# Attention and MLP in one kernel: the high half-precision parts of q, k and v made on DVE instead of POOL, with eleven scheduling constants replaced

## The chip, the core and the metric

The kernel runs on one core of one Trainium2 chip. A core has a matrix engine (PE), a vector engine (DVE), a scalar engine (ACT), a further vector processor (POOL) and an engine that here does nothing but issue DMAs (SP). Each engine runs its own list of instructions strictly in order and waits on semaphores for the others. The metric is device time in microseconds (us) of one execution.

## The reference

Batch 8, 12 heads, 448 positions, head size 64, so a model width of 768; hidden width 3072; float32 in and out.

```
scores = q @ k^T / sqrt(64) - log(448)          # per batch and head
x      = sigmoid(scores) @ v                     # heads laid side by side: 448 x 768
u      = x + (x^T @ U @ V)^T                     # rank 32, mixes the 448 positions
out    = u + relu(u @ w_ch1) @ w_ch2             # 768 -> 3072 -> 768
```

There is no softmax: the sigmoid needs no sum over a row.

## The kernel before, in words

**Numbers.** PE multiplies float16. To keep near-float32 precision, a float32 matrix x is scaled by a power of two s and split into a high part hi = float16(s*x) and a low part lo = float16(s*x - hi). A product then takes three matmuls: hi*hi, hi*lo and lo*hi. Making hi takes one input tensor (a multiplication by s); making lo takes two (x and hi). Batches 0 and 1 do their attention in plain float32, which is slower on PE but needs no split; batches 2 to 7 use the three-matmul form.

**Work and stages.** A "pair" is two heads of one batch, 448 positions: it loads q, k and v, computes scores (line 503), a sigmoid on ACT (line 590), a split of the sigmoid (lines 611 and 363) and the product with v (lines 514 and 518). Six pairs make a batch, after which the low-rank mixing follows (`mix` and `mix_half`). In stretches:

- about 0 to 300 us: attention of batches 0 and 1, and `decode`: the weights come as 64-bit words, are turned to float32, split, and stored to DRAM (`scratch`).
- about 300 to 950 us: the MLP of batches 0 to 3 (`ffn_in` line 838, `ffn_out` line 858), while the attention of batches 2 to 7 runs in between.
- about 950 us to the end: the MLP of batches 4 to 7, two batches at a time, by a scheme that multiplies quarters of the matrices with seven products in place of eight (`in_quad`, `out_quad`, product at line 1031). It needs sums of weight quarters, which `quarter_sums` makes: four additions and four more on POOL (lines 917 and 921), a cast on ACT (line 924), a subtraction on DVE (line 925) and a store. One buffer holds the sums, so a group on POOL starts only when the subtraction of the group before it is done. Eight groups run before 950 us, sixteen after.
- `far_forms` makes the sums of u for the first two of those batches ahead of time and stores them to DRAM (`ufar`, line 974); `near_forms` loads them back (line 998).

In `in_quad`, each product's results are combined and split again on DVE for the next stage. Near its end stands a row of seven DVE instructions that mostly read two tensors from SBUF (lines 1060, 363, 363, 1069, 1069, 1069, 363). The text calls this row a **burst**.

**What sets the order.** Nothing is emitted where it is written. Each step is registered with `op(engine, cost, function, reads, writes, position)`. `Plan.order` then walks a nominal clock: it always takes the operation that could start earliest by the nominal costs, and among those ready on one engine the one with the smallest position. That list, fixed at build time, is the order of each engine. Two more rules matter. An operation with `port=True` may not overlap another such one in the nominal clock: POOL operations with inputs have it, and so do the DVE operations registered through `dve2`; those of `in_quad` and `out_quad` are registered through `dve`, without it. And tiles come from rings of buffers, granted in that nominal time: `stg`, which holds the six parts of q, k and v of a pair, has two buffers.

**The preparation of a pair** (batches 2 to 7, function `pair`): ACT bounds q, k and v (line 420); the three bounds go by DMA through DRAM to every partition (`far`, `row`); DVE takes the largest (line 399), POOL computes inverse scales (`inv`, and the small factors `c` and `cv`), DVE the scales (line 403). Then, on POOL, the high parts of k, q and v are made by `scaled` (line 360 of the helper `ts`), and on DVE the low parts by `rest` (line 363).

The table of constants at lines 59 to 67 sets positions: `BEFORE`, `PREP`, `MIX_2`, `A_OFF` and so on shift the positions of attention, preparation, mixing and the split of the sigmoid; `ROOM0` and `ROOM` the nominal room left between batches; `U_STEP` and `STEP_K` the spacing of `far_forms` and of `quarter_sums`.

Of the kernel before, what the change touches and what calls it, by code (L numbers as in the profile page):

```python
# [32 lines left out]
ALU = mybir.AluOpType  # L33
# [22 lines left out]
FORMS = {1: (0,), 2: (1,)}  # L56
MM = 0.190

ROOM0, ROOM, AHEAD, BEFORE, PACE = 42.52, 45.6, 46.05, 25.79, 0.95
PREP, BOUNDS, VALUES, SECOND, MIXED = 14.886, 8, 1.353, 2.168, 6.146  # L60
LOW_POOL = ()
MIXED1, MIX_1 = 6.47, 3.6
MIX_2, EV_IN, EV_OUT, A_OFF = 1.824, 21.322, 5.63, 0.0
START, DECODE = 59.033, 39.61
U_AT, U_STEP = 4.779, 5
LEAD, SUMS, STEP_K, STEP_I, FFN_LEAD = 35.115, 18.57, 22.57, 8.637, 4.0
ORDER = "iiiioiooiioiooiioiooiooo"


# [19 lines left out]
class Plan:  # L89
# [13 lines left out]
    def op(self, eng, cost, fn, reads=(), writes=(), pos=0.0, slack=0.0, land=0.12, after=(), port=False):  # L103
        deps = set(after)
        for k in reads:
            deps.update(self.wrote.get(k, ()))
        for k in writes:
            deps.update(self.wrote.get(k, ()))
            deps.update(self.read.get(k, ()))
        i = len(self.ops)  # L110
        for k in reads:
            self.read.setdefault(k, []).append(i)
        for k in writes:
            self.wrote[k], self.read[k] = [i], []
        tiles = []
        for k in (*reads, *writes):
            t = k[0] if isinstance(k, tuple) else k
            if isinstance(t, Tile) and t not in tiles:
                tiles.append(t)
                t.users.append(i)  # L120
                if t.at is None:
                    t.at = (pos, i)
        self.ops.append((eng, cost, fn, sorted(deps), pos, slack, land, tiles, port))
        return i
# [96 lines left out]
def fused_kernel(ctx: ExitStack, tc: tile.TileContext, q, k, v, wu, wv, w1, w2, out):  # L221
    nc = tc.nc
    B = q.shape[0]
    plan = Plan()
# [109 lines left out]
    def sm(name, n, ring_=3):  # L334
        if name not in small:
            small[name] = ring(name, ring_, [n], F32)
        return plan.tile(name, small[name])
# [7 lines left out]
    def dve2(cost, fn, reads, writes, pos):  # L345

        op("DVE", cost, fn, reads, writes, pos, port=True)
# [4 lines left out]
    def pool(cost, fn, reads, writes, pos, after=()):  # L352
        op("POOL", cost, fn, reads, writes, pos, after=after, port=bool(reads))
# [4 lines left out]
    def ts(eng, out, in_, s1, op0, s2=None, op1=None):  # L358
        kw = {} if op1 is None else {"op1": op1}
        eng.tensor_scalar(out=out, in0=in_, scalar1=s1, scalar2=s2, op0=op0, **kw)  # L360
# [4 lines left out]
    def scaled(out, in_, s):  # L365
        ts(nc.gpsimd, out, in_, s, ALU.mult, 1.0, ALU.mult)
# [159 lines left out]
    def pair(b, p, at, d):  # L526
        whole = b < WHOLE
        u32, mx = u32s[b], mxs[b]
        if b == 0:
            qk, v32, kqk = loads(b, p, at - 60.0)  # L530
        else:
            qk, v32, kqk = loads(b, p, at - d - (30.0 if whole else 32.0))
        tiles, keys = {}, []
        if whole:
            c, kc = 1.0 / math.sqrt(D), []

            def score_products():
                return [(qk.x[:, 1, :], qk.x[:, 0, :])]

            def value_products():  # L540
                return [(v32.x, lambda t, h: t.x[:, h * S : (h + 1) * S])]

            kscore, kvalue = kqk, [v32]
        else:
            prep = at - PREP
            st, ss = plan.tile("stg", STG), sm("ss", 3)
            for i in range(2):
                bound(lambda i=i: qk.x[:, i, :], S, lambda i=i: ss.x[:, i : i + 1], kqk[2 * i : 2 * i + 2], (ss, i), prep - BOUNDS, 0.73)
            bound(lambda: v32.x.rearrange("p a b -> p (a b)"), 512, lambda: ss.x[:, 2:3], [v32], (ss, 2), prep - BOUNDS, 0.82)
            s, inv = scale_by_dma(ss, [(ss, i) for i in range(3)], 3, "qkv", prep - BOUNDS + 1)  # L550
            cc, cv = sm("c", 1), sm("cv", 1)
            pool(0.5, lambda: ts(nc.gpsimd, cc.x, inv.x[:, 0:1], inv.x[:, 1:2], ALU.mult, 1.0 / math.sqrt(D), ALU.mult), [inv], [cc], prep + 1)
            pool(0.45, lambda: ts(nc.gpsimd, cv.x, inv.x[:, 2:3], 1.0 / A_UP, ALU.mult, 1.0, ALU.mult), [inv], [cv], prep + 1)

            def part(n):

                if n < 4:
                    n = (2, 3, 1, 0)[n]
                    return st.x[:, n * S : (n + 1) * S]
                return st.x[:, 4 * S + (n - 4) * 4 * P : 4 * S + (n - 3) * 4 * P].rearrange("p (a b) -> p a b", a=4)  # L560

            for i in (1, 0):
                ki = kqk[2 * i : 2 * i + 2]
                pool(0.7, lambda i=i: scaled(part(2 * i), qk.x[:, i, :], s.x[:, i : i + 1]), ki + [s], [(st, 2 * i)], prep + 2,
                     plan.wrote["decoded"])
                dve2(0.63, lambda i=i: rest(part(2 * i + 1), qk.x[:, i, :], s.x[:, i : i + 1], part(2 * i)),
                    ki + [s, (st, 2 * i)], [(st, 2 * i + 1)], prep + 3)
            pool(0.8, lambda: scaled(part(4), v32.x, s.x[:, 2:3]), [v32, s], [(st, 4)], prep + 6, plan.wrote["decoded"])
            dve2(0.75, lambda: rest(part(5), v32.x, s.x[:, 2:3], part(4)), [v32, s, (st, 4)], [(st, 5)], prep + 7)

            def score_products():
                kh, kl = st.x[:, S:], st.x
                return [(kh, part(0)), (kh, part(1)), (kl, part(0))]

            def half(t, x):

                n = t.x.shape[1]
                return t.x.bitcast(F16)[:, x * n : (x + 1) * n]

            def value_products():  # L580
                def side(x):
                    return lambda t, h: half(t, x)[:, h * S : (h + 1) * S]

                return [(part(4), side(0)), (part(5), side(0)), (part(4), side(1))]

            kscore, kvalue = [(st, i) for i in range(4)], [(st, 4), (st, 5)]
            c, kc = cc, [cc]

        def sigmoid(cost, out_, in_, rows, pos, kin, kout):
            act(cost, lambda: nc.scalar.activation(  # L590
                out_(), in_(), AF.Sigmoid, bias=bias_s[rows], scale=c if whole else c.x[rows]), kin + ["bias"] + kc, kout, pos)

        sc = {}
        for n, j in enumerate((3, 0, 1, 2)):
            here = at + (d * (n // 2) / SECOND if b else 0.0)
            if b == 0:
                sc = scores_of(b, (j,), score_products, kscore, here, b == 0 or b == 1 and p < 2)
            elif n % 2 == 0:
                sc = scores_of(b, ((3, 0), (1, 2))[n // 2], score_products, kscore, here, b == 0 or b == 1 and p < 2)
            a = tiles[j] = plan.tile(*(("a1", A1) if j == 3 else ("a2", A2)))  # L600
            to = a if whole else plan.tile(*(("t1", AT1) if j == 3 else ("t2", AT2)))
            for h in range(2):
                rows = rows_of(h) if j == 3 else slice(0, P)
                cols = slice(0, S) if j == 3 else slice(h * S, h * S + S)
                sigmoid(0.66 if whole else 0.72, lambda to=to, rows=rows, cols=cols: to.x[rows, cols],
                        lambda h=h, sc=sc, j=j, rows=rows: sc[j, h].x[rows, :S], rows, here, [sc[j, h]], [(to, h)])
            kto = [(to, h) for h in range(2)]
            if whole:
                keys += kto
                continue  # L610
            act(0.57 if j == 3 else 0.95, lambda a=a, to=to: nc.scalar.activation(half(a, 0), to.x, AF.Copy, scale=A_UP), kto, [(a, 0)], here + A_OFF)  # L611
            dve2(0.63 if j == 3 else 1.16, lambda a=a, to=to: rest(half(a, 1), to.x, A_UP, half(a, 0)), kto + [(a, 0)], [(a, 1)], here + A_OFF)
            keys += [(a, 0), (a, 1)]
        late = at + d * (VALUES if b else 1.0)
        av = values_of(b, value_products, tiles, keys + kvalue, late)
        ku = u32[p]
        act(0.63, lambda: nc.scalar.activation(u32[p].x, av.x[:, :S], AF.Copy, scale=1.0 if whole else cv.x),
            [av] + ([] if whole else [cv]), [ku], late)
        if b > 0:
            largest(lambda: u32[p].x, lambda: mx.x[:, p : p + 1], [ku], (mx, p), late)  # L620
# [671 lines left out]
```

## Time and profile before

| quantity | value |
|---|---|
| median of 3 runs | 1598.71 us (1597.11 to 1600.68) |
| profiled execution, its own time | 1600.42 us |
| profiled execution, span of the instructions | 1598.6 us |
| PE busy | 1563.9 us, 98% |
| DVE busy | 1163.3 us, 73% |
| ACT busy | 855.8 us, 54% |
| POOL busy | 385.4 us, 24% |
| chain of work that ended last | PE 82%, DVE 9%, DMA 4%, the rest below 3% each |

A row of a group reads: line, engine, operation, output<-inputs, shapes, count, then busy us, mean ns of one, idle time of the engine before them and what ended it. Matmul ends are modelled and overlap their successors, so "PE busy" says that work was in flight, not that each slot was used; what PE waited for stands in the view of waits.

### The profile page before, as it was taken

The numbers are of one execution on the slowest core, as the hardware profiler recorded it, in microseconds if no ns is written. First come the engines' busy times: TensorE is split into PE (matmuls) and PEld (weight loads), VectorE is DVE, ScalarE is ACT, GpSimd is POOL, SyncE is SP. The second block draws the span as 40 slices with busy tenths as digits, with TensorE's granted clock in tenths as the row PEclk, the third lists the DMA queues.
The fourth block names the chain that finished last, engine by engine and source line by source line (L and its number), as shares of the span: only waits on it lengthen the run. The fifth ranks groups of instructions, "written<-read, shape, count | busy, mean of one in ns | idle before, by whom it ended". The sixth has DMA issues, their size and how long they took to land.

```text
span 1598.6 us, 23902 instructions
## 1 busy us (share of the span) xinstructions
PE 1563.9 (98%) x8774; PEld 769.3 (48%) x8774; DVE 1163.3 (73%) x1887; ACT 855.8 (54%) x1553; POOL 385.4 (24%) x468
## 2 busy tenths in 40 slices
PE   8999999999999999999999999999998999999999
PEld 3344444444454444454444444544444545555554
DVE  3899898666766568767677776797888777565656
ACT  6667754567846679757877872332333514121210
POOL 0100002642213442211211210466665320000000
PEclk9999999999999999999999999999999999999999
DMA  8798896765665797866766648877676663333321
GB/s 246 246 319 280 293 310 209 277 209 144 166 191 147 241 220 215 206 189 181 218 178 200 175 146 255 261 246 221 206 230 219 219 223 130 131 105 119 124 104 70
DMA packets 217430, 322.53 MB, mean 202 GB/s; under 512 B 132832, under 2 KB 183392, under 8 KB 205024
## 3 DMA queue, kind: packets, MB, share of 16 engines
q1 hardware_dynamic: 217312, 321.01, 65.1%
q8 instruction: 68, 1.11, 0.3%
q14 instruction: 50, 0.41, 0.1%
HBM read 249.40 MB, written 77.42 MB: 204 GB/s over the span
## 4 chain that ended last, share of the span: by engine, by line
PE 82%; DVE 9%; DMA 4%; ACT 2%; SPq 1%; issue 1%; POOL 1%; ACTq 0%; DVEq 0%; POOLq 0%
PE bank L1031 28%; PE bank L838 18%; PE bank L858 18%; PE bank L503 8%; PE bank L518 5%; PE bank L514 2%; DVE us__88 L363 1%; DMA qk__99<-q_in 1%; DVE xnt L925 1%; DVE us__87 L1069 1%; PE bank L755 1%; SPq L747 1%; DMA forms<-xnt 1%; DMA far<-ss__213 1%; DVE h__94 L363 1%
## 5 line engine op out<-in xcount | busy, mean ns | idle before, releaser
L363 DVE SCALAR_TENSOR_TENSOR a<-at,a 128x896 f16<-128x896 f32 (+1 forms) x144 | 143.1, 1000 | 44.5 <-ACT a L611 44.3
L858 PE MATMUL bank<-h__94,w__92 128*128 128x448 f16 x864 | 173.1, 353 | 1.4 <-DVE a L363 0.9
L858 PE MATMUL bank<-h__93,w__91 128*128 128x448 f16 x864 | 173.1, 353 | 0.0
L611 ACT ACTIVATE a<-at 128x896 f16<-128x896 f32 (+1 forms) x144 | 123.1, 855 | 0.5
L838 PEld LDWEIGHTS <-w__89 128*128 128x128 f16 x864 | 82.8, 98 | 84.0 <-issue 9.3
L838 PEld LDWEIGHTS <-w__90 128*128 128x128 f16 x864 | 83.5, 98 | 82.5 <-issue 8.3
L858 PEld LDWEIGHTS <-w__92 128*128 128x128 f16 x864 | 82.4, 98 | 83.9 <-issue 10.6
L858 PEld LDWEIGHTS <-w__91 128*128 128x128 f16 x864 | 81.4, 98 | 82.3 <-issue 9.8
L1031 PEld LDWEIGHTS <-w__89 128*128 128x128 f16 x819 | 80.1, 98 | 80.0 <-issue 5.4
L921 POOL TENSOR_TENSOR w<-w 128x384 f32<-128x384 f32 x96 | 110.4, 1150 | 5.2
L1031 PEld LDWEIGHTS <-w__91 128*128 128x128 f16 x756 | 74.4, 98 | 74.5 <-issue 6.4
L1031 PEld LDWEIGHTS <-w__90 128*128 128x128 f16 x756 | 73.9, 98 | 73.7 <-issue 5.0
L1031 PEld LDWEIGHTS <-w__92 128*128 128x128 f16 x693 | 68.3, 99 | 69.5 <-issue 7.3
L917 POOL TENSOR_TENSOR w<-w 128x384 f32<-128x384 f16 x64 | 66.1, 1060 | 116.0 <-DVE xnt L925 62.1
L838 PE MATMUL bank<-us__87,w__90 128*128 128x448 f16 x432 | 86.5, 357 | 0.9 <-DVE ua__78 L363 0.9
L838 PE MATMUL bank<-us__87,w__89 128*128 128x448 f16 x432 | 85.0, 353 | 1.2 <-ACT h__93 L846 1.2
L838 PE MATMUL bank<-us__88,w__90 128*128 128x448 f16 x432 | 85.8, 353 | 0.0
L838 PE MATMUL bank<-us__88,w__89 128*128 128x448 f16 x432 | 85.6, 353 | 0.0
L590 ACT ACTIVATE at<-bank,bias_s,c__226 128x448 f32<-128x448 f32 (+1 forms) x96 | 67.0, 725 | 14.9 <-PE bank L503 11.2
L590 ACT ACTIVATE at<-bank,bias_s,c__224 128x448 f32<-128x448 f32 (+1 forms) x96 | 66.8, 724 | 8.0 <-PE bank L503 5.2
L590 ACT ACTIVATE at<-bank,bias_s,c__225 128x448 f32<-128x448 f32 (+1 forms) x96 | 66.3, 721 | 4.6 <-PE bank L503 2.5
L590 ACT ACTIVATE a<-bank,bias_s 128x448 f32<-128x448 f32 (+1 forms) x96 | 55.9, 630 | 10.7 <-PE bank L503 10.1
(1190 smaller groups left out, 3122.0 us busy)
## 6 DMA issues: line engine op xcount, KB each, us to landing
w<-w_in SPq DMA_DIRECT2D x48, 768.0 KB, 5.8
forms<-xnt SPq DMA_DIRECT2D x24, 768.0 KB, 4.2
w__89<-forms SPq DMA_DIRECT2D x13, 1344.0 KB, 6.0
w__90<-forms SPq DMA_DIRECT2D x12, 1344.0 KB, 6.2
w__91<-forms SPq DMA_DIRECT2D x12, 1344.0 KB, 5.9
w__92<-forms SPq DMA_DIRECT2D x11, 1344.0 KB, 6.0
forms<-scratch SPq DMA_DIRECT2D x144, 96.0 KB, 4.8
w__89<-scratch SPq DMA_DIRECT2D x9, 1536.0 KB, 7.7
```

The costliest lines, as they stand in the source:

```text
L363: nc.vector.scalar_tensor_tensor(out=out, in0=in0, scalar=s, in1=in1, op0=op0, op1=op1)
L503: nc.tensor.matmul(o, keys, y[rows_of(h)], start=i == 0, stop=i == n - 1)
L514: nc.tensor.matmul(av.x[:, :S], x[:, 3, :], y(tiles[3], 0), start=i == 0, stop=False, skip_group_check=True)
L518: nc.tensor.matmul(av.x[rows_of(h), :S], x[:, j, rows_of(h)], y(tiles[j], h), start=False, stop=j == 2 and i == n - 1, skip_group_check=True,)
L590: act(cost, lambda: nc.scalar.activation(out_(), in_(), AF.Sigmoid, bias=bias_s[rows], scale=c if whole else c.x[rows]), kin + ["bias"] + ...
L611: act(0.57 if j == 3 else 0.95, lambda a=a, to=to: nc.scalar.activation(half(a, 0), to.x, AF.Copy, scale=A_UP), kto, [(a, 0)], here + A_OFF)
L747: op("SP", 1.0, lambda: nc.sync.dma_start_transpose(out=xt.x, in_=xs.x.rearrange("p c x s -> p (c x s)")), [(xs, i, x) for i in range(3) f ...
L838: nc.tensor.matmul(ph.x[:, :S], wx[:, x, c, f * P : (f + 1) * P], us.x[:, c, y, :], start=c == 0 and i == 0, stop=c == NP - 1 and i == 2,)
L858: nc.tensor.matmul(po.x[:, :S], wx[:, x, f, e * P : (e + 1) * P], h.x[:, f, y, :], start=f == 0 and i == 0, stop=f == FC - 1 and i == 2,)
L917: pool(1.0, lambda j=j: nc.gpsimd.tensor_tensor(out=t.x[:, j], in0=quarter(j, 0), in1=quarter(j, 1), op=ALU.add), [(w, j, 0), (w, j, 1)] i ...
L921: pool(1.0, lambda o_=o_, x=x, y=y, sub=sub: nc.gpsimd.tensor_tensor(out=t.x[:, o_], in0=t.x[:, x], in1=t.x[:, y], op=ALU.subtract if sub ...
L1031: nc.tensor.matmul(bank.x[:, :S], wt.x[:, k, FACTOR[n], x], both(f)[:, y], start=start and k == i == 0, stop=k == 2 and i == 2, skip_group ...
```

## The change

Two things are changed. First, 108 instructions move: for each of the 36 pairs of batches 2 to 7, the high parts of k, q and v are made by a `tensor_scalar` on DVE, registered through `dve2`, and no longer by one on POOL. They lose their explicit dependence on the end of `decode`. Second, eleven constants that set nominal positions get other values; since the order is found by a list walk, instructions then stand elsewhere on every engine, in all stages.

```diff
-ROOM0, ROOM, AHEAD, BEFORE, PACE = 42.52, 45.6, 46.05, 25.79, 0.95
-PREP, BOUNDS, VALUES, SECOND, MIXED = 14.886, 8, 1.353, 2.168, 6.146
+ROOM0, ROOM, AHEAD, BEFORE, PACE = 43.26, 50, 46.05, 29.9, 0.95
+PREP, BOUNDS, VALUES, SECOND, MIXED = 14.175, 8, 1.353, 2.168, 6.146
 LOW_POOL = ()
-MIXED1, MIX_1 = 6.47, 3.6
-MIX_2, EV_IN, EV_OUT, A_OFF = 1.824, 21.322, 5.63, 0.0
-START, DECODE = 59.033, 39.61
-U_AT, U_STEP = 4.779, 5
-LEAD, SUMS, STEP_K, STEP_I, FFN_LEAD = 35.115, 18.57, 22.57, 8.637, 4.0
+MIXED1, MIX_1 = 6.334, 3.6
+MIX_2, EV_IN, EV_OUT, A_OFF = 1.226, 21.185, 5.63, -7.16
+START, DECODE = 59.033, 40.9
+U_AT, U_STEP = 4.779, 4.877
+LEAD, SUMS, STEP_K, STEP_I, FFN_LEAD = 35.115, 18.57, 23.046, 8.637, 4.0
...
             for i in (1, 0):
                 ki = kqk[2 * i : 2 * i + 2]
-                pool(0.7, lambda i=i: scaled(part(2 * i), qk.x[:, i, :], s.x[:, i : i + 1]), ki + [s], [(st, 2 * i)], prep + 2,
-                     plan.wrote["decoded"])
+                dve2(0.4, lambda i=i: ts(nc.vector, part(2 * i), qk.x[:, i, :], s.x[:, i : i + 1], ALU.mult), ki + [s], [(st, 2 * i)], prep + 2)
                 dve2(0.63, lambda i=i: rest(part(2 * i + 1), qk.x[:, i, :], s.x[:, i : i + 1], part(2 * i)),
                     ki + [s, (st, 2 * i)], [(st, 2 * i + 1)], prep + 3)
-            pool(0.8, lambda: scaled(part(4), v32.x, s.x[:, 2:3]), [v32, s], [(st, 4)], prep + 6, plan.wrote["decoded"])
+            dve2(0.45, lambda: ts(nc.vector, part(4), v32.x, s.x[:, 2:3], ALU.mult), [v32, s], [(st, 4)], prep + 6)
             dve2(0.75, lambda: rest(part(5), v32.x, s.x[:, 2:3], part(4)), [v32, s, (st, 4)], [(st, 5)], prep + 7)
```

Below line 565 the changed kernel's line numbers are one smaller: its line 924 is line 925 of before.

Place 1, DVE in the preparation of one pair in the middle stretch. `stg` holds the parts, `qk` and `v` the inputs, `a<-at` is the split of a sigmoid, `e`, `inv` and `s_qkv` belong to the scales. Before:

```order
L399 TENSOR_REDUCE e_qkv__217<-row__120 128x3
L360 TENSOR_SCALAR e_qkv__217<-e_qkv__217 128x3
L363 SCALAR_TENSOR_TENSOR ua__78<-bank_112,kg__181,ua__78 128x448
L403 RECIPROCAL s_qkv__223<-inv_qkv__220 128x3
L363 SCALAR_TENSOR_TENSOR a<-at,a 128x448
L424 TENSOR_REDUCE mx__231<-ub__86 128x1
L774 TENSOR_REDUCE mm_x__199<-mx__231 128x1
L363 SCALAR_TENSOR_TENSOR a<-at,a 128x896
L363 SCALAR_TENSOR_TENSOR stg__109<-qk__100,s_qkv__222,stg__109 128x448 x2
L377 TENSOR_REDUCE e_x__202<-bank_110 1x1
L363 SCALAR_TENSOR_TENSOR stg__109<-v__103,s_qkv__222,stg__109 128x512
```

The same pair in the change:

```order
L399 TENSOR_REDUCE e_qkv__217<-row__120 128x3
L360 TENSOR_SCALAR e_qkv__217<-e_qkv__217 128x3
L403 RECIPROCAL s_qkv__223<-inv_qkv__220 128x3
L363 SCALAR_TENSOR_TENSOR a<-at,a 128x448
L363 SCALAR_TENSOR_TENSOR a<-at,a 128x896
L360 TENSOR_SCALAR stg__109<-qk__100,s_qkv__222 128x448 x2
L363 SCALAR_TENSOR_TENSOR stg__109<-qk__100,s_qkv__222,stg__109 128x448
L424 TENSOR_REDUCE mx__231<-ub__86 128x1
L363 SCALAR_TENSOR_TENSOR stg__109<-qk__100,s_qkv__222,stg__109 128x448
L773 TENSOR_REDUCE mm_x__199<-mx__231 128x1
L360 TENSOR_SCALAR stg__109<-v__103,s_qkv__222 128x512
L846 TENSOR_TENSOR h__93<-r__95,h__93 128x448
```

The three `TENSOR_SCALAR ... stg` rows, which stood on POOL, now stand between DVE's own rows; the rest of the preparation keeps its neighbours nearly as they were.

Place 2, SP's queue just before the quarter scheme starts. `ufar<-w` are the stores of `far_forms`, `a`, `stg` and `at<-ufar` the loads of `near_forms`, the transpose belongs to `mix_half`. Before:

```order
L998 DMA qk__101<-ufar 128x448
L998 DMA v__105<-ufar 128x448
L998 DMA a<-ufar 128x448 x3
L747 DMA_TRANSPOSE w_107<-w_107 128x21x128
L998 DMA a<-ufar 128x448 x4
L998 DMA stg__108<-ufar 128x448 x2
L974 DMA ufar<-w_107 128x448
L998 DMA stg__108<-ufar 128x448
L974 DMA ufar<-w_107 128x448
L340 DMA w__90<-forms_0_131 128x5376
L998 DMA at<-ufar 128x448
```

The change:

```order
L973 DMA ufar<-w_107 128x448
L997 DMA qk__101<-ufar 128x448
L997 DMA v__105<-ufar 128x448
L997 DMA a<-ufar 128x448 x5
L746 DMA_TRANSPOSE w_107<-w_107 128x21x128
L997 DMA a<-ufar 128x448 x2
L997 DMA stg__108<-ufar 128x448 x3
L997 DMA at<-ufar 128x448
```

The last store to `ufar` stood two rows ahead of the load of `at`, behind the transpose; now it is issued ahead of the transpose, with thirteen DMAs between it and that load.

Place 3, DVE in the quarter scheme, at the ninth burst: the subtraction of `quarter_sums` (`xnt<-w,xnt`) and what stands up to the burst. Before, the burst (from line 1060 on) follows it at once:

```order
L925 TENSOR_TENSOR xnt<-w_107,xnt 128x12x128
L1060 TENSOR_TENSOR at<-h__94,r__96 128x448
L363 SCALAR_TENSOR_TENSOR us__88<-a,h__94 128x448
L363 SCALAR_TENSOR_TENSOR us__87<-a,at 128x448
L1069 TENSOR_TENSOR h__94<-at,h__94 128x448
L1069 TENSOR_TENSOR a<-us__88,a 128x448
L1069 TENSOR_TENSOR r__95<-us__87,r__95 128x448
```

The change:

```order
L924 TENSOR_TENSOR xnt<-w_107,xnt 128x12x128
L363 SCALAR_TENSOR_TENSOR h__94<-stg__109,h__94 128x448
L1083 TENSOR_TENSOR a<-a 128x448
L363 SCALAR_TENSOR_TENSOR h__93<-bank_115,fg,stg__109 128x448
L363 SCALAR_TENSOR_TENSOR r__96<-bank_116,fg,stg__109 128x448
L363 SCALAR_TENSOR_TENSOR a<-h__93,a 128x448
L1059 TENSOR_TENSOR us__88<-us__87,a 128x448
L363 SCALAR_TENSOR_TENSOR w_107<-stg__109,us__87 128x448
L363 SCALAR_TENSOR_TENSOR a<-stg__109,us__88 128x448
L1068 TENSOR_TENSOR a<-us__88,a 128x448
```

Five rows now stand between the subtraction and the ninth burst. At the other bursts the number of rows between the last subtraction and the burst moves too, up at some and down at others.

## The prediction

> **What bounds the kernel now.** I read the busy shares first, then the same by stretches, then what PE waited for in each of them.
>
> ```profile
> PE 1563.9 (98%) x8774; PEld 769.3 (48%) x8774; DVE 1163.3 (73%) x1887; ACT 855.8 (54%) x1553; POOL 385.4 (24%) x468
> ```
>
> The stretches from 60 us on, start:end, with busy us of PE, PE's weight loads, DVE, ACT and POOL, the granted clock, the DMA share and GB/s:
>
> ```profile
> 60.00:300.00 240.00, 232.13 (x1174) 111.32 (x1173) 217.97 (x401) 145.14 (x285) 26.79 (x36) 0.99 0.84 278
> 300.00:950.00 650.00, 649.53 (x4073) 315.84 (x4071) 462.50 (x774) 479.78 (x871) 188.80 (x272) 1.00 0.67 190
> 950.00:1300.00 350.00, 331.32 (x1742) 169.68 (x1742) 276.94 (x368) 121.64 (x198) 164.24 (x147) 0.99 0.72 228
> 1300.00:1598.60 298.60, 294.98 (x1560) 152.35 (x1557) 178.13 (x295) 66.88 (x120) 0.00 (x0) 1.00 0.35 123
> ```
>
> PE's waits in the middle (two rows, 300 to 950 us), then all but the smallest in the quarter scheme (950 to 1300 us); each row gives the total, the count and the longest:
>
> ```profile
> PE bank L764 <- DVE xnt L363: 0.3, 1, 0.3
> PE bank L503 <- ACT at L590: 0.2, 1, 0.2
> ```
>
> ```profile
> PE bank L1031 <- DVE ub__84 L363: 9.3, 4, 3.0
> PE bank L1031 <- DVE a L363: 3.1, 1, 3.1
> PE bank L1031 <- DVE h__94 L360: 2.0, 1, 2.0
> PE bank L1031 <- DMA at<-ufar: 1.8, 1, 1.8
> PE bank L1031 <- DVE ub__86 L363: 1.5, 1, 1.5
> PE bank L858 <- DVE a L363: 0.9, 1, 0.9
> ```
>
> The reader is to see three things. PE is the limit nearly everywhere: it waits 0.5 us of the 650 us in which the 108 moved instructions run, so that stretch can give back 0.5 us at most. The waits are in 950 to 1300 us: 9.3 + 3.1 + 2.0 + 1.8 + 1.5 + 0.9 = 18.6 us, one on a DMA and the rest on DVE, where none of the moved instructions stands; only the new constants reach it. And 60 to 300 us has 240 - 232.1 = 7.9 us without work in flight. The last stretch, 0.3 ms of matmuls, has nothing to gain.
>
> **Why DVE is late in the quarter scheme.** These are the nine bursts of the quarter scheme that overlap a `quarter_sums` group, by the same columns (DVE is the third busy time, POOL the fifth):
>
> ```profile
> 1022.70:1031.50 8.80, 8.58 (x46) 4.31 (x45) 8.80 (x10) 4.11 (x7) 4.87 (x5) 1.00 0.92 321
> 1039.70:1046.00 6.30, 6.30 (x35) 3.28 (x34) 6.17 (x10) 3.82 (x6) 0.45 (x1) 1.00 0.86 222
> 1057.80:1068.50 10.70, 9.21 (x50) 4.68 (x48) 10.70 (x12) 3.36 (x6) 9.84 (x8) 1.00 0.84 240
> 1077.50:1088.10 10.60, 8.61 (x42) 4.17 (x41) 10.53 (x13) 3.53 (x5) 5.22 (x5) 0.92 0.52 172
> 1116.30:1125.80 9.50, 9.34 (x50) 4.76 (x49) 9.35 (x11) 4.20 (x8) 5.81 (x5) 1.00 0.71 210
> 1132.80:1141.60 8.80, 6.87 (x37) 3.44 (x36) 8.80 (x12) 3.39 (x5) 4.70 (x4) 1.00 0.65 212
> 1169.30:1179.50 10.20, 8.73 (x47) 4.44 (x46) 10.20 (x12) 3.37 (x6) 7.24 (x7) 1.00 0.84 256
> 1194.20:1204.90 10.70, 7.55 (x41) 3.82 (x40) 10.59 (x12) 3.43 (x6) 9.82 (x8) 1.00 0.87 244
> 1211.60:1221.80 10.20, 7.19 (x39) 3.61 (x37) 10.20 (x12) 3.36 (x6) 7.19 (x6) 1.00 0.80 251
> ```
>
> With POOL at work a burst takes about 10 us; the second, nearly alone, takes 6.3 us. One row inside and one outside such a time, of the same line and shape (start, us, engine, line):
>
> ```profile
> 1218.10 1.41 DVE L1069 TENSOR_TENSOR at<-us__88,at 128x448 f16<-128x448 f32 x1
> ...
> 1252.18 0.61 DVE L1069 TENSOR_TENSOR h__93<-us__88,h__93 128x448 f16<-128x448 f32 x1
> ```
>
> So a DVE instruction with two SBUF inputs takes 1.41 us while POOL works and 0.61 us else. In-order DVE then empties PE's banks late. POOL lies over these bursts for 4.87 + 0.45 + 9.84 + 5.22 + 5.81 + 4.70 + 7.24 + 9.82 + 7.19 = 55.1 us, and the waits on DVE are 16.8 us: 0.30 us of PE per us of overlap, as an estimate.
>
> **The change part by part.**
>
> *The moved instructions.* On POOL the six k and q groups are 72 instructions and the v groups 36, all inside the 188.8 us of the middle stretch. What they cost on DVE has a row of the same form, and a wider one:
>
> ```profile
> L360 DVE TENSOR_SCALAR vst<-vraw,s_uv__161 128x448 f16<-128x448 f32 x1 | 0.4, 443 | 0.0
> ```
>
> ```profile
> L360 DVE TENSOR_SCALAR us__88<-w 128x768 int32<-128x768 int32 x15 | 8.0, 548 | 1.3 <-DMA w<-w_in 1.3
> ```
>
> By the first: 72 x 0.443 = 31.9 us, and for v 36 x 0.443 x 512/448 = 18.2 us, together 50.1 us. By the second, scaled by width, 0.548 x 448/768 = 0.32 us and 0.365 us, together 36 us. I take 50, since that row has the form itself. A part comes back: `rest` on q and k ran beside POOL in some pairs and not in others.
>
> ```profile
> L363 DVE SCALAR_TENSOR_TENSOR stg__109<-qk__101,s_qkv__223,stg__109 128x448 f16<-128x448 f32 x12 | 9.3, 810 | 0.0
> ...
> L363 DVE SCALAR_TENSOR_TENSOR stg__108<-qk__100,s_qkv__222,stg__108 128x448 f16<-128x448 f32 x12 | 7.7, 675 | 0.0
> ```
>
> At most 810 - 675 = 135 ns in each of 72, under 10 us. DVE thus goes from 462.5 to between 490 and 513 us of 650, 75 to 79%. Its cover is PE, which is busy throughout; price on the path: 0, with a gain bounded at 0.5 us and a loss that the rivals price.
>
> *The end of `far_forms`.* PE's wait on `at<-ufar` ends a row of SP's queue (start, us to issue):
>
> ```profile
> 976.95 4.37 SPq L747 DMA_TRANSPOSE w<-w  x1
> ...
> 989.72 0.38 SPq L974 DMA_DIRECT2D ufar<-w  x1
> ...
> 992.65 0.32 SPq L998 DMA_DIRECT2D at<-ufar  x1
> ```
>
> The last store stands behind the transpose, and the load of `at` is issued 2.9 us after it. In the change the last store is issued ahead of that transpose and thirteen DMAs ahead of the load. I take the whole 1.8 us off. Bounds: -1.8, or 0 if another load of that row is then last.
>
> *The quarter scheme.* Nothing is removed there; what can change is how bursts and POOL groups lie. A group follows the subtraction of the group before it (line 925), so the number of DVE rows between a subtraction and the next burst tells the overlap. Before, from the windows: 0 rows, 9.8 us (twice); 3 or 4 rows, 7.2; 5 rows, 5.8; 6 rows, 4.7 and 5.2; the subtraction inside the burst, 4.9; 13 rows, 0.45. In the change's order on DVE the nine bursts have 3, 6, 4, inside, 7 and then inside, 0, 5, 5 and 6 rows: 7.2 + 5.0 + 7.2 + 4.9 + 4.5 + 9.8 + 5.8 + 5.8 + 5.0 = 55.2 us, where 4.5 for the fifth is my reading between neighbours. That is the overlap of before, 55.1 us. So: 0, with bounds of -8 (half of 16.8) and +5 (0.30 x 17 more us, four bursts moved onto a subtraction).
>
> *The first 300 us.* PE's order is the same up to about 130 us; behind that the attention of batch 1 and the pieces of the MLP of batch 0 are dealt anew, around the same number of mixing steps. The longest of PE's waits there:
>
> ```profile
> PE bank L684 <- DVE xnt L363: 1.6, 1, 1.6
> ```
>
> DVE is at 218 of 240 us, decoding, and neither gains nor loses work there. I take 0, bounds -3 and +3 (twice the longest wait, either way).
>
> *Sum.* 1600.42 (own time of the profiled execution, 1.8 us of it outside the span) + 0 - 1.8 + 0 + 0 = 1598.6 us. That execution lies 1.7 us above the median of the three, 1598.71, so in terms of the median: **1596.9 us**.
>
> The granted clock is 0.99 in 950 to 1300 us: 3.5 us of half-paced work in sum, and 0.92 in the window at 1077.5, whereas the one at 1211.6, with its 3 us wait, has 1.00. [...]
>
> **The rivals.**
>
> *Better luck with the bursts.* If bursts fall into POOL's pauses, 8 us go with the 1.8 and half of the lost clock (1.7): 1598.7 - 11.5 = 1587; a third of it, the more likely size, gives 1592. For: the counts of rows are coarse against waits of 1 to 3 us, and all waits but one hang on this. Against: POOL's 164 us in the stretch are unchanged, and my count gives the old overlap.
>
> *DVE blocks in the middle.* A moved instruction needs a free `stg` buffer, which the products with v release two pairs back. On POOL that wait was long:
>
> ```profile
> POOL stg__109 L360 <- PE bank L518: 61.5, 12, 11.9
> POOL stg__108 L360 <- PE bank L518: 59.3, 12, 11.6
> ```
>
> There it harmed nobody. On DVE it holds up what is queued behind it: the splits of the sigmoid and of the hidden layer, and the additions that empty PE's banks (`ua<-bank`). PE has three banks there; a filling takes
>
> ```profile
> 597.76 3.40 PE bank L838 x18
> ```
>
> so 3.4 us for 18 matmuls and two thirds of that, 2.3 us, for the 12 of `ffn_out`; three last about 8.5 us. From a wait of 9 us on, PE stops: the two longest, 11.9 and 11.6 us, would cost 3 us each, plus 1.7 each for the clock: 1598.7 + 9 = 1608; one of them, 1603. For: DVE's share rises. Against: DVE's own work before each moved row, which mostly waits for PE itself, uses up most of the wait, and the mean wait is 121/24 = 5 us.
>
> [...]
>
> *The move does nothing at all*, the DMA wait included: another late load takes its place, 1598.7.
>
> **How the numbers follow.** Forecast 50%, its own range 1593 to 1600; better luck 24%; DVE blocks 23%; nothing 3%. What a measurement can tell from no change is 0.2%, 3.2 us, so below 1595.5 or above 1601.9. Of the forecast's 50, 17 lie below, 31 within, 2 above; better luck lies all below; blocking 22 above and 1 within; nothing, within. Faster 0.41, the same 0.35, slower 0.24. The range that leaves a fifth out reaches to a good part of both rivals: 1588 to 1605.
>
> **What would show it.** Right: PE's wait on `at<-ufar` is gone; the middle stretch still shows PE waiting about 0.5 us, with DVE at 490 to 513 us and POOL near 98; the bursts at about 10 us and waits on DVE near 17 us in the quarter scheme. Wrong: rows with DVE as releaser of PE in 300 to 950 us above 3 us in sum (blocking), or fewer than 10 us of waits behind the bursts (luck), or a first 300 us that is longer or shorter by more than 3 us.

## The result and the profile after

The changed kernel took 1610.39 us (median of 8 runs, 1606.43 to 1615.49), the kernel before 1600.51 us beside it: 1.0069 of it, 95% interval 1.0053 to 1.0085. It is slower by about 11 us by that ratio, where 1596.9 us and a gain of 1.8 us had been forecast. Its profiled execution took 1611.88 us, with a span of 1610.1 us.

The first row is the busy shares of the changed kernel; then the same stretches as before (busy us of PE, PE's weight loads, DVE, ACT and POOL, the granted clock, DMA share, GB/s):

```profile
PE 1569.9 (98%) x8774; PEld 770.1 (48%) x8774; DVE 1193.6 (74%) x1995; ACT 854.6 (53%) x1553; POOL 297.9 (19%) x360
```

```profile
60.00:300.00 240.00, 230.44 (x1157) 110.19 (x1158) 218.52 (x406) 147.46 (x289) 24.97 (x34) 0.98 0.84 276
300.00:950.00 650.00, 642.02 (x3993) 310.44 (x3992) 481.75 (x862) 466.39 (x852) 103.64 (x168) 0.99 0.68 189
950.00:1300.00 350.00, 335.30 (x1785) 171.65 (x1784) 279.10 (x371) 133.44 (x218) 166.29 (x147) 1.00 0.70 224
1300.00:1610.10 310.10, 306.44 (x1620) 158.32 (x1618) 187.61 (x311) 66.84 (x120) 0.00 (x0) 1.00 0.37 129
```

POOL lost 85 us in the middle stretch and DVE gained 19, the way the change points. But PE, which stood for 0.5 us of that stretch before, now stands for 650 - 642.0 = 8.0 us, and its clock there falls from 1.00 to 0.99. The stretch from 60 to 300 us loses 1.7 us of PE (230.4 for 232.1), the quarter scheme wins 4.0 (335.3 for 331.3). What PE waits for (a bank is one of the buffers that PE's products go to and that another engine empties), in the middle (300 to 950 us) and then from 1010 us on (total, times, longest; behind line 565 the changed kernel's numbers are one lower than before's):

```profile
PE bank L754 <- ACT at L589: 5.6, 2, 3.1
PE bank L763 <- DVE xnt L363: 2.0, 1, 2.0
PE bank L763 <- ACT at L589: 0.3, 1, 0.3
```

```profile
PE bank L1030 <- DVE ub__84 L363: 6.4, 3, 2.4
PE bank L1030 <- DVE us__87 L363: 4.9, 3, 2.5
PE bank L1030 <- DVE us__88 L363: 1.7, 1, 1.7
PE bank L1030 <- ACT a L1067: 1.1, 1, 1.1
PE bank L1030 <- DVE a L1068: 0.7, 1, 0.7
```

The wait on `at<-ufar` is gone. The new waits in the middle are three: 2.5 and 3.1 us for ACT's sigmoid, 2.0 us for the low part of the mixed tile `xnt`. Here is the first, on ACT and then PE (start, us, engine, line; in brackets the idle time before it and what ended it):

```profile
434.23 0.95 ACT L610 ACTIVATE a<-at 128x896 f16<-128x896 f32 x1
443.31 0.58 ACT L420 ACTIVATE junk<-qk__101 128x448 bf16<-128x448 f32 x1 [8.14 <-DMA qk__101<-k_in]
...
444.73 2.21 ACT L589 ACTIVATE at<-bank,bias_s,c__226 64x448 f32<-64x448 f32 x3
```

```profile
445.50 0.65 PE L754 MATMUL bank<-w,ua 128*128 128x384 f16 x3 [2.51 <-ACT at L589]
```

ACT stood for 8.14 us at the bound of one pair's k, since the load of k had not landed. Behind it in ACT's row stood the sigmoids whose banks PE needed. In the kernel before, the loads of this pair are there hardly any sooner, but its bounds stand behind those sigmoids, and the first of them waits 0.35 us, for the load of q:

```profile
438.02 2.22 ACT L590 ACTIVATE at<-bank,bias_s,c__226 64x448 f32<-64x448 f32 x3 [1.19 <-PE bank L503]
...
444.21 0.58 ACT L420 ACTIVATE junk<-qk__101 128x448 bf16<-128x448 f32 x1 [0.35 <-DMA qk__101<-q_in]
```

At 682 and 812 us it is the same: a bound waits 5.75 and 4.31 us for its load, and a sigmoid, or the cast of `xnt` that stands right behind the bound, comes late. The place in ACT's row is not all that changed: the loads of these pairs also take longer from issue to landing. Here is the first pair, before and changed:

```profile
DMA to landing us min/median/max: 2.8/2.9/3.0
```

```profile
DMA to landing us min/median/max: 5.8/6.0/9.1
```

At the second and third places the medians are 5.5 and 10.4 us, where the kernel before has 4.4 and 3.3 for the same pairs. At the first place they were issued earlier (from 436.1 for 439.4 us) and were there hardly any sooner. With the old landing times the first hold would be some 3 us shorter and the third would not be there: an estimate from these rows. Why the loads are slower was not tested.

Each of the three waits of PE is followed by a stretch of 3.41 us at a granted clock of 0.50 (from 446.06, 684.99 and 814.70 us). The table of stretches, cut at the times at which the clock changes, around the second:

```profile
678.17:681.59 3.42, 3.42 (x25) 1.60 (x24) 0.00 (x0) 0.00 (x0) 0.00 (x0) 1.00 0.63 156
681.59:685.00 3.41, 0.42 (x3) 0.10 (x1) 0.51 (x1) 2.75 (x7) 0.00 (x0) 1.00 0.98 395
685.00:688.41 3.41, 3.30 (x10) 1.32 (x9) 1.67 (x4) 3.36 (x7) 0.00 (x0) 0.50 0.89 260
688.41:691.83 3.42, 3.42 (x27) 1.73 (x27) 3.13 (x6) 1.07 (x3) 0.00 (x0) 1.00 0.52 116
```

PE is idle for most of the second row and runs at 0.50 in the whole of the third, so it loses 1.7 us more. The middle stretch thus costs 7.5 us of waits and 3 x 1.7 = 5.1 us of clock, 12.6 us: more than the whole loss.

### The profile page after: what moved, and what is told of

It reads as the page before. It is cut to its first block, busy times and chain, and to the rows that moved or that the text cites. A ratio compares the mean times of both kernels' runs of the same rounds, so it can differ in the third digit from the quotient of the medians.

```text
span 1610.1 us, 23764 instructions
## 1 busy us (share of the span) xinstructions
PE 1569.9 (98%) x8774; PEld 770.1 (48%) x8774; DVE 1193.6 (74%) x1995; ACT 854.6 (53%) x1553; POOL 297.9 (19%) x360
## 4 chain that ended last, share of the span: by engine, by line
PE 80%; DVE 8%; issue 3%; POOL 3%; DMA 3%; ACT 2%; SPq 0%; POOLq 0%; DVEq 0%; ACTq 0%
PE bank L1030 24%; PE bank L837 20%; PE bank L857 18%; PE bank L503 8%; PE bank L518 5%; PE bank L514 2%; POOL w L920 2%; POOL w L916 1%; PE bank L754 1%; DVE a L363 1%; DMA qk__101<-k_in 1%; DMA qk__101<-q_in 1%; DMA w<-w_in 1%; PE bank L382 0%; DVE stg__108 L363 0%
```

## The experiments

Two theories. **A, the order:** the planner, charged otherwise and with other constants, dealt the rows anew, and in three pairs ACT's bound came to stand ahead of sigmoids while its load was still on the way; the 108 instructions on DVE cost no time. **B, the load:** DVE, with 50 us more, is late with what PE needs.

Beside each ratio (to the kernel before on the same chip, 95% interval) stand two means over its runs: the span times the mean granted clock, taken as the time at full clock, and the span times one less that clock, taken as what half clock lost (so it is if PE has work all through the stretches at half clock). Before, they are 1590.6 to 1590.8 and 6.1 to 7.7 us in the three comparisons that list the clocks of both; the changed kernel has 1597.0 and 11.5. Single runs of one kernel lie up to 9 us apart in the first of these means too; its standard error is 0.3 to 0.9 us where there are seven runs or more and 0.5 to 1.4 us where there are four, so a difference of 1 us in that column says nothing.

| kernel | median us | ratio (interval) | at full clock | lost |
|---|---|---|---|---|
| changed | 1610.39 | 1.0069 (1.0053 to 1.0085) | 1597.0 | 11.5 |
| changed order, on POOL | 1609.41 | 1.0061 (1.0039 to 1.0083) | 1596.1 | 10.4 |
| old order, on DVE | 1599.22 | 1.0007 (0.9988 to 1.0026) | 1591.3 | 6.4 |
| changed, three bounds later | 1601.38 | 1.0015 (1.0003 to 1.0027) | 1591.5 | 7.5 |
| changed code, old constants | 1609.58 | 1.0074 (1.0059 to 1.0089) | 1595.8 | 11.7 |
| old code, new constants | 1603.28 | 1.0024 (1.0008 to 1.0040) | 1590.9 | 11.1 |
| old, one bound earlier | 1602.90 | 1.0024 (1.0008 to 1.0041) | 1593.1 | 9.0 |
| old, two bounds earlier | 1608.09 | 1.0069 (1.0048 to 1.0090) | 1594.8 | 12.9 |
| old, POOL's sums left out | 1585.91 | 0.9910 (0.9881 to 0.9939) | 1576.8 | 7.1 |
| old, POOL's sums on DVE | 1592.83 | 0.9953 (0.9938 to 0.9968) | 1585.4 | 6.0 |
| old, half of the sums on DVE | 1600.48 | 1.0015 (1.0003 to 1.0028) | 1589.1 | 10.4 |
| old order, sums and high parts on DVE | 1593.72 | 0.9977 (0.9962 to 0.9991) | 1585.9 | 6.4 |
| changed, bounds later and sums on DVE | 1600.63 | 1.0008 (0.9991 to 1.0026) | 1591.7 | 7.0 |

### Order and engine apart

The changed kernel's rows, with the instructions given to POOL; and the old kernel's rows, with the instructions given to DVE (the planner's charge stays as it was in each):

```diff
 # changed order, on POOL
-dve2(0.4, lambda i=i: ts(nc.vector, part(2 * i), qk.x[:, i, :], s.x[:, i : i + 1], ALU.mult), ...
+dve2(0.4, lambda i=i: scaled(part(2 * i), qk.x[:, i, :], s.x[:, i : i + 1]), ...
 # old order, on DVE
-pool(0.7, lambda i=i: scaled(part(2 * i), qk.x[:, i, :], s.x[:, i : i + 1]), ...
+pool(0.7, lambda i=i: ts(nc.vector, part(2 * i), qk.x[:, i, :], s.x[:, i : i + 1], ALU.mult), ...
```

(and the same for v)

> The changed kernel's order of instructions on every engine, but the 108 moved instructions (high parts of q, k and v) execute on POOL again. Theory A (the re-dealt order costs the time: in three pairs ACT's bound stands in its queue before its q or k load has landed, and the sigmoids and casts behind it free PSUM banks late): about as the changed kernel, 1606 to 1613 us, and PE still waits 2 to 3 us for ACT at L589 near 443, 682 and 811 us. Theory B (the 108 instructions load DVE, and what DVE does later costs the time): back to 1598 to 1603 us, with those waits gone.

> The old kernel's order on every engine, with the 108 instructions executed on DVE. Theory A: within 3 us of the old kernel (1597 to 1604 us), no wait of PE over 2 us between 300 and 950 us; DVE is some 50 us busier there and POOL some 70 to 100 us less. Theory B: 1606 us or more, with waits of PE for DVE between 300 and 950 us.

The order carries the loss: 1.0061 without a single moved instruction on DVE, 1.0007 with all of them there. PE's waits in the middle, of the changed order on POOL and of the old order on DVE:

```profile
PE bank L754 <- ACT at L589: 4.8, 2, 3.4
PE bank L763 <- DVE xnt L363: 2.1, 1, 2.1
```

```profile
PE bank L376 <- DVE mm_x__197 L774: 0.3, 1, 0.3
PE bank L503 <- ACT at L590: 0.2, 1, 0.2
```

The first kernel has the three waits at the same places, the second has none of them. Theory B falls. The slow landing goes with the order as well: the loads of the three pairs take 5.9, 5.5 and 10.8 us (medians) in the first kernel and 2.8, 3.4 and 3.3 us in the second.

### The three bounds alone

The changed kernel, with the bounds of three pairs a few rows later:

```diff
+if 6 * LATER.index(b) + p in (11, 23, 29):
+    plan.late.append(([first, first + 1, first + 2, first + 3], 6))   # three bounds, one store
 def emit(self):
-    for i in self.order():
+    # each op of plan.late goes up to 6 ACT instructions later, never past its own users
```

> The changed kernel; in three pairs of the middle (the 12th, 24th and 30th of the 36) the three bounds on ACT and the store of the pair's sums stand up to six ACT instructions later; nothing else moves on DVE, PE or POOL. Theory A: the three waits of PE for ACT near 443, 682 and 811 us go (2.5 + 3.1 + 2.0 us) and with them the three stretches at half clock (about 1.7 us each): 10 to 13 us below the changed kernel, 1597 to 1601 us. Theory B: no change, 1606 to 1613 us. In between (1601 to 1606 us): the waits are part of the cause, and delaying these bounds makes another wait.

What is left of PE's waits in the middle is one row:

```profile
PE bank L391 <- DVE e_u__240 L369: 0.4, 1, 0.4
```

Nine bounds on ACT and three stores on SP were moved, and 1.0069 became 1.0015. The loads of these pairs land as late as in the changed kernel (medians 6.7, 5.6 and 10.7 us), so the place in ACT's row is what makes PE wait for them. At full clock the kernel is back at 1591.5 us, 5.5 us below the changed one, and the half clock loses 7.5 us in place of 11.5. What is left is 0.15%, 2.4 us, a little more than was expected for theory A (1601.38 us, where 1597 to 1601 was named); the waits of the first 300 us stay as the changed kernel has them.

### The same wait put into the old kernel

```diff
+if 6 * LATER.index(b) + p in (11, 23, 30):
+    plan.early.append((len(plan.ops) - 3, 8))       # the first bound, up to 8 ACT instructions earlier
 # second kernel: the first and the second bound
+    plan.early += [(len(plan.ops) - 3, 8), (len(plan.ops) - 2, 8)]
```

> The old kernel; in three pairs of the middle the first of the three bounds stands up to eight ACT instructions earlier, ahead of three or four sigmoids (L590 in the old kernel's lines). Nothing else moves on any engine; the loads are issued where they were. Theory A: ACT waits 5 to 8 us at each of them for its q or k load (near 437, 676 and 807 us), PE then waits 2 to 4 us for a bank at each, with a stretch at half clock after it: 8 to 16 us more than the old kernel, 1606 to 1615 us. Theory B (a late bound on ACT is not what PE feels): within 3 us of the old kernel.

> The old kernel, with the first two of the three bounds of the same three pairs up to eight ACT instructions earlier (with the first alone, only one of the three met a load that had not landed: ACT idle for 7.6 us, PE for 3.8 us, then 6.8 us at half clock, and 1.0024 of the old kernel). Theory A: the second bound needs the later half of the load, so ACT is held 4 us or more in at least two of the three, and the time grows with the number of PE waits, 3 to 6 us for each: 1605 to 1616 us. If the time does not grow beyond that of the first alone although PE waits in two or three places: theory A is short of a part.

The dose was smaller than meant. Of the first kernel, at the first of the three places, on ACT and on PE:

```profile
442.59 0.58 ACT L428 ACTIVATE junk<-qk__101 128x448 bf16<-128x448 f32 x1 [7.64 <-DMA qk__101<-q_in]
```

```profile
443.92 1.28 PE L522 MATMUL bank<-a,stg__109 128*128 128x448 f16 x3 [3.80 <-ACT at L600]
```

In the other two pairs (the third is the 31st of the 36 here, not the 30th) the bound was moved too far: it stands ahead of the loads of its own pair, so it waits for no load and reads what the buffer held before. At the second place, on ACT and in SP's queue:

```profile
678.97 0.58 ACT L428 ACTIVATE junk<-qk__101 128x448 bf16<-128x448 f32 x1
```

```profile
681.77 1.03 SPq L348 DMA_DIRECT2D qk__101<-k_in  x1
```

At the third, the bound runs at 811.1 us and the first load is issued at 812.2. In the second kernel both bounds of these two pairs stand ahead of their loads in the same way. So one hold of ACT was put in, not three, in either kernel, and even there some loads of the pair are issued behind the moved bounds, for which SP's queue then stands up to 2.1 us in the first kernel and 3.6 us in the second. That one hold does what theory A says: 7.6 us on ACT, 3.8 us on PE, and 1.0024. The second kernel has the one hold too (PE waits 4.1 us) and took 1.0069. Its mean at full clock is 4.2 us above before's, about that wait, but its four runs lie between 1591.6 and 1597.4; the other 6.5 us are half clock, 12.9 us lost where the first kernel lost 9.0. Why it lost so much more there is not settled. Neither kernel is the test of three waits that was meant, and theory A rests on the two kernels that part order and engine and on the three bounds alone.

### Constants or charge

```diff
 # changed code, old constants: the table of lines 59 to 66 as before
 # old code, new constants: pool(0.7, ...) and pool(0.8, ...) with the changed table
```

> The changed code (the planner charges the 108 instructions to DVE) with the old kernel's table of constants. If the new constants carry the loss: within 5 us of the old kernel, 1596 to 1606 us. If the planner's charge to DVE alone re-deals the order badly: 1606 us or more. Theory A names either by the same mark: PE waits for ACT at L589 between 300 and 950 us where the loss is, none where it is not.

> The old code (high parts on POOL, the planner charges POOL) with the new table of constants. The changed code with the old constants took 1.0074 of the old kernel's time, so the charge to DVE alone re-deals the order badly. If the new constants were a tuning for that charge and carry no loss of their own: within 5 us of the old kernel. If each of the two re-deals the order by chance, and most orders are worse than the tuned one: 1604 us or more here too, with waits of PE for ACT or DVE in the middle or in the quarter scheme that the old kernel does not have.

Neither alone gives PE the three waits that the two together give. PE's waits in the middle, of the charge alone and of the constants alone (the two longest rows of each):

```profile
PE bank L376 <- DVE mm_x__199 L773: 2.6, 1, 2.6
PE bank L763 <- DVE xnt L363: 0.8, 1, 0.8
```

```profile
PE bank L764 <- ACT at L590: 0.6, 1, 0.6
PE bank L764 <- DVE xnt L363: 0.4, 1, 0.4
```

With the charge alone, 1.0074, the loss is in other places: 4.7 us of PE in the middle and, by the rows of the quarter scheme, 19.5 us of waits there in place of 17.0. With the constants alone, 1.0024, the time at full clock is the old one, 0.3 us more, and the loss is half clock. The new constants bring the 1.8 us lost in 60 to 300 us (PE busy 230.1 us with them alone, 230.4 in the changed kernel, 232.0 and 232.1 without). So the three deals lose 4, 11 and 12 us in three different ways. In the changed kernel it is not the moved instructions, and with the new constants alone none is moved; with the charge alone, order and engine were not parted.

### What POOL's sums cost the quarter scheme

The prediction counted 0.30 us of PE's time for each us that POOL's additions lie over a burst of DVE. In the first kernel these additions are left out (fills and additions of 24 columns in their place); in the second and third all eight, or the first four, run on DVE at their old place:

```diff
 # left out
-nc.gpsimd.tensor_tensor(out=t.x[:, j], in0=quarter(j, 0), in1=quarter(j, 1), op=ALU.add)
+nc.gpsimd.memset(t.x[:, j], 0.01)
 # on DVE (line 917, all four of a group; and line 921 for all eight)
-nc.gpsimd.tensor_tensor(...)
+nc.vector.tensor_tensor(...)
```

> The old kernel, but POOL's eight additions of each quarter sum are left out (four constant fills and four additions of 24 columns stand in their place), so that one of the seven forms of each weight is wrong. It measures what POOL's additions cost the quarter scheme. If DVE's operations on two operands in SBUF are slowed beside them (1.33 to 1.42 us in place of 0.61) and that is what PE waits for: those go to 0.61 us throughout, most of the 18.4 us of waits of PE for DVE between 1020 and 1310 us go, with the stretches at half clock there: 1576 to 1584 us. If the waits come from DVE's own load: 1594 us or more.

> The old kernel's order, with POOL's eight additions of each quarter sum executed on DVE at the same place. DVE gets 128 more instructions of about 0.55 us after 950 us (70 us more, on top of 240 of 290 busy), less the slowing, about 0.75 us for each of the some 45 operations that ran beside POOL (34 us). If the slowing is worth more than the load: below the old kernel, 1580 to 1596 us. If the added instructions stand ahead of the operations that PE waits for: 1600 us or more, with PE's waits for DVE in the quarter scheme longer than 2 to 3 us each.

> The old kernel's order, with only the first four of the eight additions of each quarter sum on DVE; the second four stay on POOL. If what is won goes with the time that POOL works beside DVE's operations: about half of it, 0.997 to 0.998 of the old kernel, 1594 to 1597 us. If the place of the second four beside the operations that PE waits for decides: as the old kernel, within 2 us of it, or as all eight on DVE, 0.995.

Without the sums the two-operand rows of DVE that took 1.3 to 1.4 us take 0.61 to 0.66, one wait of the quarter scheme is left, and 9 in 1000 of the time goes:

```profile
PE bank L1031 <- DVE ub__84 L363: 2.8, 1, 2.8
```

So 14 us is what the sums on POOL cost in all, 13.8 of it at full clock (two runs). That is the most that the overlap can cost, for this kernel is also spared what waits for the sums themselves. With the sums on DVE about half of that is won, 1592.83 us, below both kernels. The groups of the additions there (950 to 1310 us; columns as before: busy us, mean ns of one), and the longest rows of PE's waits:

```profile
L921 DVE TENSOR_TENSOR w<-w 128x384 f32<-128x384 f32 x64 | 35.2, 550 | 0.3
L917 DVE TENSOR_TENSOR w<-w 128x384 f32<-128x384 f16 x64 | 34.7, 549 | 2.4 <-DMA w<-scratch 2.4
```

```profile
PE bank L1031 <- DVE ub__84 L363: 7.3, 4, 2.8
PE bank L1031 <- DVE a L363: 1.1, 1, 1.1
PE bank L1031 <- DVE h__94 L360: 1.1, 1, 1.1
```

An addition takes 0.55 us on DVE. On POOL, in the kernel before, the same ones took twice that, beside two-operand rows of DVE of 1.3 to 1.4 us that take 0.61 to 0.66 without them:

```profile
L921 POOL TENSOR_TENSOR w<-w 128x384 f32<-128x384 f32 x64 | 74.9, 1170 | 3.8
L917 POOL TENSOR_TENSOR w<-w 128x384 f32<-128x384 f16 x64 | 66.1, 1060 | 116.0 <-DVE xnt L925 62.1 <-DMA w<-scratch 53.9
```

DVE takes on 70 us of additions there, of which only 21 us show (245.0 to 266.3 us busy from 1010 to 1310 us), and it is less in PE's way, since nearly all its additions and subtractions of two operands for the bursts stay at 0.61 to 0.63 us. That it stands ahead of the emptying of banks in places shows in the waits that remain. Half of the sums wins nothing (1.0015): the groups' second halves then lie over the bursts, whose two-operand rows again take 1.0 to 1.4 us in part, and two waits have grown to 4.1 and 4.2 us.

### Both together

> The old kernel's order with both the 108 high parts and the additions of the quarter sums on DVE. If both are as neutral or as useful as they were alone: 0.994 to 0.998 of the old kernel, 1589 to 1597 us. If DVE, with some 120 us more work than in the old kernel, becomes the bound somewhere: slower than with the additions alone by 5 us or more, with waits of PE for DVE between 700 and 1020 us.

> The changed kernel with the three late bounds and, besides, the quarter sums' additions on DVE in place of POOL. The late bounds alone left 1.0015 of the old kernel, the additions on DVE alone 0.9953. If the two causes are separate and add: about 1.0015 - 0.0047 = 0.997 of the old kernel, 1593 to 1598 us, with the waits of PE between 1020 and 1310 us down from 14.4 to some 9 us. If the changed kernel's order in the quarter scheme leaves no room for them: 1600 us or more.

In the old order the high parts cost nothing at full clock beside the sums on DVE: 1585.9 us, beside 1585.4 with the sums alone. By the plain ratio half of the gain is gone, 0.9977 for 0.9953; the rest of that difference is half clock (before lost 6.4 us in the one comparison and 7.7 in the other). In the changed order, with the bounds mended, the gain does not come: 1.0008, at full clock 1591.7. In its profile the quarter scheme has some 6 us less of waits than with the bounds alone, but PE loses 4.0 us more from 60 to 300 us (226.7 us busy for 230.8) and 1.4 in the middle. Sums stand between DVE's rows there, ahead of one that PE waits for:

```profile
PE bank L391 <- DVE e_w__190 L369: 2.5, 1, 2.5
```

The smaller waits were not followed up one by one. Causes that were separate in place were not separate in DVE's row.

## Why the prediction was wrong, step by step

- **The moved instructions cost DVE some 50 us and the path nothing: right; what comes back was sized too small.** The rows measure 0.446 us for q and k and 0.479 for v, 72 x 0.446 + 36 x 0.479 = 49.4 us where 50.1 was worked out, and the old order with all of them on DVE took 1.0007 (0.9988 to 1.0026). But DVE's busy time in the middle came to 481.8 us, not 490 to 513: over the whole run it rose by 30.3 us (1163.3 to 1193.6), so 19 us came back where under 10 had been counted. Line 363 gave 10 of them; the rest was not traced.
- **The end of `far_forms`, -1.8 us: right** in the profile; between 950 and 1010 us PE waits for nothing.
- **The quarter scheme at 0, bounds -8 and +5: right within its bounds.** The waits went from 17.0 to 14.8 us. That POOL's overlap causes them was right; the price of it, 0.30 x 55 = 16.8 us, measured 14, for the sums as a whole.
- **The first 300 us at 0, bounds of 3: within its bounds** by the waits, a loss of 1.7 us. A stretch at half clock there was also twice as long in this execution (6.83 us from 254.9 us, before 3.41), another 1.7 us, which the old order on DVE has too.
- **The middle at 0: the step that failed.** "Its cover is PE, which is busy throughout; price on the path: 0, with a gain bounded at 0.5 us and a loss that the rivals price." The stretch cost 12.6 us in the profiled execution. The cover was there for the work that the prediction looked at, DVE's, and that work did need no more. But the change also moved rows on ACT, and on SP in this stretch, and these were not read: of ACT's row the prediction says nothing. The rival that comes nearest, "DVE blocks in the middle", had the stretch and the shape right, and the size nearly (1603 to 1608 us): an instruction at the head of an in-order row that waits for something far away while those that empty PE's banks queue behind it. It named the wrong engine and the wrong wait: ACT's bound and a load, not DVE's high part and an `stg` buffer. That its size came near the measured 1610 us is luck. The rows for it stood in the trace of before: the loads of `qk__101`, the last of which ends ACT's wait there at 444.21 us, and the instructions of ACT from 435 us to it, which the new order has behind it.
- **The price of a wait** in that rival, 3 us and 1.7 us of half clock, was right in kind: 2.0 to 3.1 us, and 1.7 us for each. No row of the prediction shows that 1.7 us. It is half of a stretch of 3.41 us at 0.50, of which the kernel before has two in the quarter scheme (from 1086.33 and 1287.72 us) and the changed kernel one after each of the three waits.

## What to carry to other kernels

When constants or costs of a planner change, the instructions that were meant to move can be the smallest part, as here: read every in-order row in which something waits for a load, and ask for each such waiter whether it now stands ahead of something that the busiest engine needs. A slack of a few us at such a place was worth more here than an engine's share of busy time, and one kernel with the old order and the new engine, one with the new order and the old engine, tell the two apart at once. A slow engine beside a fast one can cost more than the work it takes off: here POOL's additions (1.06 to 1.17 us each on POOL, 0.55 on DVE), in the old order, were better done by the engine that was already the busier (0.9953); in the new order the gain did not come (1.0008, where the bounds alone gave 1.0015).

## What the runs showed of the hardware

**From 300 us on, half clock followed the intervals in which PE was busy least.** In the profiled executions of the two kernels the stretches at 0.50 are 3.41 us long, one of the changed kernel's 6.83 us, and within one execution they start whole multiples of 3.413 us apart: at 69.16, 250.07, 1086.33 and 1287.72 us before, at 70.59, 254.91, 446.06, 684.99, 814.70 and 1067.28 us in the changed kernel (one that starts within the last 0.4 us of either span is left out). With the time from 300 us on divided at that spacing, the six intervals that a stretch at 0.50 followed have PE busy for 1.42 and 1.04 us before (from 1082.92 and 1284.31 us) and for 0.91, 0.42, 1.40 and 0.89 us in the changed kernel (from 442.65, 681.59, 811.29 and 1063.87 us). The least that PE was busy in an interval that none followed is 1.60 us before (from 1137.53 us) and 1.50 us in the changed kernel (from 1292.57 us). The first 300 us are not sorted so: in the kernel before a stretch at 0.50 followed the interval from 65.75 us, in which PE is busy for 3.35 of 3.41 us, and the one from 246.65 us with 1.56 us. So standing alone does not set the clock there. In the changed kernel the interval from 254.91 us, itself at 0.50, was followed by another at 0.50 with PE busy for 2.47 us of it. Before, the longest wait of the quarter scheme, 3.1 us, cost nothing further: it lay across two intervals, with PE busy for 1.74 and 1.94 us, and the clock stayed at 1.00:

```profile
1195.60:1199.01 3.41, 3.41 (x20) 1.76 (x18) 3.41 (x4) 1.13 (x2) 3.41 (x3) 1.00 0.91 263
1199.01:1202.43 3.42, 1.74 (x10) 0.78 (x8) 3.42 (x4) 0.63 (x1) 3.26 (x4) 1.00 1.03 197
1202.43:1205.84 3.41, 1.94 (x11) 1.02 (x11) 3.29 (x6) 1.40 (x3) 1.87 (x2) 1.00 0.85 354
1205.84:1209.25 3.41, 3.41 (x20) 1.76 (x19) 3.41 (x5) 2.22 (x3) 0.00 (x0) 1.00 0.01 3
```

The changed kernel's wait of 3.1 us in the middle lay almost whole in one interval, the one from 681.59 us, and cost the 1.7 us more. How often a wait falls in the one way or the other was not counted.

**Half clock makes part of the spread.** The same kernel's runs lie over 10 us apart (1595 to 1606 us before). Within the kernels of the table, what half clock lost goes with the span by a correlation of 0.72, about half of the variance. The product of span and granted clock is not steady from run to run: in 25 runs of the kernel before on one chip it spreads as widely as the span does (standard deviations 2.5 and 2.4 us). Its means over 19 to 25 runs agree to 0.2 us from one comparison to the next (1590.6 to 1590.8), which is closer than their standard errors of 0.3 to 0.5 us and so in part luck. Read beside the plain time and with these errors, it helps to tell a wait of PE from luck with the stretches at half clock.
